# Two attention blocks on one core: where the swapped half of P is put right

## The chip, the core and the metric

The kernel runs on one core of a Trainium2 chip. The metric is the time of one execution on the device in microseconds (us), lower is better. The core has five engines with instruction queues of their own: TensorE (PE; PEld is its weight load), VectorE (DVE), ScalarE (ACT), GpSimd (POOL) and SyncE (SP, which here only issues DMAs). They meet through semaphores.

## The reference

Two attention blocks, A and B, each with its own x, K and V cache and weights, and their outputs side by side. B_x and A_x are 16 x 32 x 1024, all tensors bf16.

```python
def _A_ref(x, k_cache, v_cache, wq, wo):      # Hq = 32, Hkv = 4, Sk = 1024, Dh = 128
    q = (x @ wq).reshape(B, Sq, Hq, Dh).transpose(0, 2, 1, 3)
    k = jnp.repeat(k_cache, rep, axis=1)      # rep = 8
    v = jnp.repeat(v_cache, rep, axis=1)
    scores = jnp.einsum("bhqd,bhkd->bhqk", q, k) * (Dh ** -0.5)
    p = softmax(scores, axis=-1)
    o = jnp.einsum("bhqk,bhkd->bhqd", p, v)
    return o.transpose(0, 2, 1, 3).reshape(B, Sq, Hq * Dh) @ wo
...
return jnp.concatenate([a, b], axis=-1)       # B: the same with 32 K/V heads, no repeat
```

## The kernel before

**Work.** The main loop has 128 steps (NIT). Each does one unit of B, 4 heads of one batch (1 MB of K and 1 MB of V), and one unit of A, half of one K/V head of one batch (256 KB each of K and V for two steps). Between them lie the Q projections (qprojA, qprojB, L660), the output projections (oproj, L716) with their sums in acc (L726, L730), and the loads of the weights.

**One step of B**, in the order of the functions:

- st_dmaK, st_dmaV: SP loads K and V of the 4 heads; partition 32a+p holds 32 keys of head a. There are three slots for each.
- st_ktrB (L844): VectorE transposes K in 32x32 blocks of 4-byte pairs, in two instructions (halves g of the keys), into KBt_sb.
- st_scores (L873, L884): POOL spreads the queries over two columns (QD_sb), and PE makes the scores in 64x64 tiles, each two heads high. Row half r of the array and key half g go to column half cg = r ^ g. So in PSUM the group g=0 has heads 0, 1 on partitions 0 to 63 and heads 2, 3 on 64 to 127, and the group g=1 has them the other way round.
- st_exp (L908): ScalarE makes exp of the scores with the row sums as accumulator output (each such instruction is followed by an accumulator read). For g=0 it is one instruction on 128 partitions. For g=1 there are two on 64 partitions each, which read one half and write P_sb in the other, so that the halves are put right there. L912 ("shift") adds the two row sums on VectorE.
- st_ptr (L920): VectorE transposes P in 32x32 blocks, one instruction of 128x256 for each g, into PT_sb.
- st_pdiag (L933): POOL copies PT_sb into the block-diagonal PD_sb in four copies of 32 partitions. Each needs all of PT_sb, and PD_sb is single.
- st_pv (L981): PE multiplies with V in 64x64 tiles into the banks ps_o and ps_pt.
- st_recip (L990), st_norm (L997, L1001, L1003) and st_otr (L1008, L583): reciprocals of the sums on VectorE, ScalarE brings one bank over (OS_sb), VectorE adds and scales, PE transposes, ScalarE evacuates.

**One step of A:** scores (L862) on PE, one exp of 128x1024 (L899) on ScalarE, PV with a column of ones (L944), and every second step normalisation on VectorE (L954, L956). POOL copies V of A into the tile with the ones (VAp_sb, L819), which frees VA_sb for the next load on SP.

**Order.** The program is first written step by step; then list_schedule puts all operations in an order for each engine by estimated durations (DUR), the longest remaining path, and constants found by tuning (BONUS for each kind of operation, LOOK, A_LEAD, SWITCH_WEIGHT, DMA_MARGIN, SP_AHEAD, slowdown factors). The orders are fixed in the program. Waits are derived from names of buffers and parts of buffers, such as ("P", g, o) or ("PT", g). A second, general program (after L339) runs only where the row sums leave the range, and doesn't run here.

Of the kernel before, what the change touches and what calls it, by code (L numbers as in the profile page):

```python
# [7 lines left out]
ALU = alu_op_type.AluOpType  # L8
ACTF = mybir.ActivationFunctionType
# [10 lines left out]
LAZY_PER_STEP = 100  # L20
LAZY_DELAY = 0
A_STEPS_FRAC = 1.0
LOOK = 0.052
A_LEAD = 577.882
BONUS = {
    "KBt_tr": -157.6, "KTA_ev@act": -282.6, "KTA_ev@dve": -7.6, "KTA_tr": 104.7, "OT_ev@act": 98.0,
    "OT_evA@dve": 194.3, "OT_tr": 55.0, "OT_trA": -66.0, "PD_cp": 120.5, "PD_ev@act": -97.1, "PT_ev@act": -350.3,
    "PT_tr": 47.6, "PT_trB": 28.6, "PVA": -87.3, "PVB": 111.0, "QD_cp": 222.8, "VAp_cp": 84.9, "acc+": 132.0,
    "acc0": 58.0, "accF": -195.1, "exp": -257.9, "expA": 163.5, "ka_dma": 8.8, "kb_dma": 6.2, "norm@dve": -607.1,
    "normA@dve": 228.1, "oprojA": 121.3, "oprojB": -188.6, "oswap": 328.6, "out_dma": 294.6, "qA_ev@act": -27.6,  # L30
    "qA_ev@dve": 383.6, "qB_ev@act": -115.9, "qB_ev@dve": -28.9, "qprojA": 90.7, "qprojB": 150.4, "recip": -7.2,
    "scoresA": -92.9, "scoresB": 19.2, "shift": 89.4, "va_dma": 146.0, "vb_dma": 2.7, "woA_dma": 224.2,
    "woB_dma": 65.7, "wq_dma": 287.0, "xT_ev@act": 434.7, "xT_ev@dve": 233.0, "xT_tr": 131.0, "x_dma": 299.4,
}
SWITCH_WEIGHT = 4.07
DMA_MARGIN = 1.043
PIECE = {"kb_dma": (32768, 32), "wq_dma": (2048, 256), "vb_dma": (32768, 32), "out_dma": (2048, 128)}
PIECE_DEFAULT = (8192, 32)
SP_COST = {"kb_dma": 0.66, "vb_dma": 0.66, "wq_dma": 0.5, "out_dma": 0.5}
SP_COST_DEFAULT = 0.63  # L40
DMA_START = 1.7
SP_AHEAD = 4.874
DMA_LAND = 0.5
DMA_SLOW = 1.06
PE_CLASS = {"scoresB": "S", "PVB": "S"}
PE_LEAVE = {"S": 0.35, "V": 0.16, "F": 0.0}
PE_ENTER = 0.22
PE_SLOW = 1.147
SEEN = {"act": 0.16, "dve": 0.13, "pool": 0.05, "pe": 0.29, "sp": 0.04}

DUR = {
# [30 lines left out]
class Prog:  # L82
# [117 lines left out]
    def list_schedule(self):  # L200
# [40 lines left out]
        while True:  # L241
            best = None
            bkey = None
            for eng, lst in ready.items():
# [6 lines left out]
                emin = min(at.values())  # L251
                ci = max([i for i in lst if at[i] <= emin + LOOK], key=lambda i: (bl[i] + BONUS.get(ops[i].name, 0.0) - SWITCH_WEIGHT * toll(i), -i))
                key = (at[ci], -bl[ci])
# [25 lines left out]
            for u in users[best]:  # L279
                uo = ops[u]  # L280
                r = op.t1 if op.eng == uo.eng == "pe" else seen
                if uo.dma_key is not None:
                    r += DMA_MARGIN
                if r > ready_t[u]:
# [189 lines left out]
def build(nc, pa, pb, out):  # L474
    P = 128
# [9 lines left out]
    scale = float(Dh) ** -0.5  # L485
# [25 lines left out]
    pr = Prog()  # L511
    with contextlib.ExitStack() as stack:
# [3 lines left out]
        def ps(name, shape, dt):  # L516
# [3 lines left out]
        stat = sb("stat", [P, 2, 4], F32)  # L520
        rinv_all = sb("rinv_all", [P, 2 * NIT], F32)
# [9 lines left out]
        acc = sb("acc", [P, 2, NG, D], F32)  # L531
# [9 lines left out]
        PT_sb = sb("PT_sb", [P, Sk // 2], F32)  # L541
# [11 lines left out]
        zeros = PT_sb[:, 0:P // 2].bitcast(BF)  # L553

        ps_s = ps("ps_s", [P, 2, 2, 512], F32)
# [6 lines left out]
        BK_S = [[("bank", 0), ("bank", 1)], [("bank", 2), ("bank", 3)]]  # L562
        BK_KT, BK_PT, BK_O, BK_PJ = ("bank", 4), ("bank", 5), ("bank", 6), ("bank", 7)

        pr.add("pool", lambda g: g.memset(zeros, 0.0), writes=["PT"], name="c0")
        pr.add("pool", lambda g: g.affine_select(ident[:], zeros, [[1, P]], ALU.not_equal, 1.0, base=0, channel_multiplier=-1),
               reads=["PT"], writes=["ident"], name="c1")
        for g in range(2):
# [131 lines left out]
        def oproj(pi, blk, G):  # L700
# [9 lines left out]
            for oh in range(NOH):  # L710
# [17 lines left out]
                else:  # L728
                    claim = ost_claim()
                    pr.add("dve", lambda e, a_ap=a_ap, o_ap=o_ap, ps_a=ps_a: e.tensor_tensor(o_ap, a_ap, ps_a[:, 0:OUTW], ALU.add),  # L730
                           reads=[bk, ("acc", pi, G, oh)] + claim["reads"], writes=[bk, ("ost", ob, oh)] + claim["writes"], name="accF", prio=A_LEAD if pi == 0 else 0.0)
                    if G == NG - 1:
# [161 lines left out]
        def st_exp(q):  # L894
            sbf = q.sbuf
            if q.pi == 0:
                src = ps_s[:, sbf, :, :].rearrange("p u n -> p (u n)")
                dst = PTA_sb[:, q.half, :, :].rearrange("p c n -> p (c n)")
                pr.add("act", lambda e: e.activation(dst, src, ACTF.Exp, scale=scale),  # L899
                       writes=BK_S[sbf] + [("PTA", q.half)], name="expA",  # L900
                       rtag={("Sv", sbf): q.qid}, wtag={("PTA", q.half): q.qid})
            else:
                st = stat[:, q.t % 2, :]
                p_out = P_sb[:, :].rearrange("p (g m j w) -> p g m j w", g=2, m=8, w=2)
                for g in range(2):
                    for o, n, r in (((0, P, 0),), ((0, 64, 64), (64, 64, 0)))[g]:
                        src = ps_s[r:r + n, sbf, g, :].rearrange("p (m w j) -> p m j w", m=8, w=2)
                        pr.add("act", lambda e, src=src, g=g, o=o, n=n: e.activation(p_out[o:o + n, g], src, ACTF.Exp, scale=scale, accum_out=st[o:o + n, g:g + 1]),  # L908
                               writes=[BK_S[sbf][g], ("P", g, o), ("rowsum", q.t % 2, g, o)], name="exp",
                               rtag={("Sv", sbf): q.qid}, wtag={("P", g, o): q.qid, ("rowsum", q.t % 2, g, o): q.qid})  # L910
                parts = [(0, 0), (1, 0), (1, 64)]
                pr.add("dve", lambda e: e.tensor_tensor(st[:, 2:3], st[:, 0:1], st[:, 1:2], ALU.add),  # L912
                       reads=[("rowsum", q.t % 2, g, o) for g, o in parts], writes=[("total", q.t % 2)], name="shift",
                       rtag={("rowsum", q.t % 2, g, o): q.qid for g, o in parts}, wtag={("total", q.t % 2): q.qid})

        def st_ptr(q):
            p32 = P_sb[:, :].bitcast(F32)
            for g in range(2):
                parts = [(0, 0)] if g == 0 else [(1, 0), (1, 64)]
                pr.add("dve", lambda e, g=g: e.transpose(PT_sb[:, 256 * g:256 * g + 256], p32[:, 256 * g:256 * g + 256]),  # L920
                       reads=[("P", g_, o) for g_, o in parts], writes=[("PT", g)], name="PT_tr",
                       rtag={("P", g_, o): q.qid for g_, o in parts}, wtag={("PT", g): q.qid})

        def st_pdiag(q):
            for a in range(4):
                src = PT_sb[32 * a:32 * a + 32, :].rearrange("p (m q) -> p m q", m=16)
                dst = PD_sb[32 * a:32 * a + 32, :, a % 2, :]
                keys = [("PD", a, g) for g in range(2)]
                if a == PD_ACT:
                    pr.add("act", lambda e, src=src, dst=dst: e.copy(dst, src), reads=[("PT", g) for g in range(2)], writes=keys, name="PD_ev@act",  # L930
                           rtag={("PT", g): q.qid for g in range(2)}, wtag={k: q.qid for k in keys})
                else:
                    pr.add("pool", lambda e, src=src, dst=dst: e.tensor_copy(dst, src), reads=[("PT", g) for g in range(2)], writes=keys, name="PD_cp",  # L933
                           rtag={("PT", g): q.qid for g in range(2)}, wtag={k: q.qid for k in keys})

        OA0 = Dh + 4

# [49 lines left out]
                       rtag=dict([(k, q.qid) for k in keys] + [(("VB", kvs), q.kid)]), wtag={"Ops": q.qid})  # L987

        def st_recip(q):
            pr.add("dve", lambda e: e.reciprocal(q.rinv, stat[:, q.t % 2, 2:3]), reads=[("total", q.t % 2)], writes=["rinv", ("rinv_all", 1)], name="recip",  # L990
                   rtag={("total", q.t % 2): q.qid}, wtag={"rinv": q.qid})

        def st_norm(q):
            st = stat[:, q.t % 2, :]
            for o in (0, 64):
                r = 64 - o
                pr.add("dve", lambda e, o=o, r=r: e.reciprocal(st[r:r + 64, 3:4], st[o:o + 64, 2:3]), reads=[("total", q.t % 2)], writes=[("rswap", q.t % 2, r)], name="recip",  # L997
                       rtag={("total", q.t % 2): q.qid}, wtag={("rswap", q.t % 2, r): q.qid})
            for o in (0, 64):
                r = 64 - o  # L1000
                pr.add("act", lambda e, o=o, r=r: e.activation(OS_sb[o:o + 64, :], ps_o1[r:r + 64, 0:Dh], ACTF.Copy, scale=st[r:r + 64, 3:4]),  # L1001
                       reads=[("rswap", q.t % 2, r)], writes=[BK_PT, ("OS", o)], name="oswap", rtag={"Ops": q.qid, ("rswap", q.t % 2, r): q.qid}, wtag={("OS", o): q.qid})
            pr.add("dve", lambda e: e.scalar_tensor_tensor(OB_sb[:, :], ps_o[:, 0:Dh], q.rinv, OS_sb[:, :], ALU.mult, ALU.add),  # L1003
                   reads=["rinv", ("OS", 0), ("OS", 64)], writes=[BK_O, "OB"], name="norm@dve", rtag={"rinv": q.qid, "Ops": q.qid, ("OS", 0): q.qid, ("OS", 64): q.qid}, wtag={"OB": q.qid})
# [168 lines left out]
        pr = pr.list_schedule()  # L1173
# [37 lines left out]
```

## Time and profile before

| what | value |
|---|---|
| time, median of 2 runs | 881.19 us (880.24 to 882.14) |
| the profiled execution | 882.14 us, of which 880.3 us are the span of the profile |
| VectorE: K transposes L844 (KB_sb, wq_sb, xT_sb) | 275.1 + 19.3 + 17.0 us |
| POOL: PD copies L933 | 311.5 us, 512 of 608 ns |
| ScalarE: accumulator reads of L908 | 50.1 + 25.1 us, 384 of 196 ns |
| ScalarE: exp of A, L899 | 131.3 us, 128 of 1025 ns |
| bytes moved | 341.82 MB, mean 388 GB/s |
| mean granted TensorE clock | 0.974 |

The page gives each engine's busy time as a share of the span, then groups of instructions by source line: "x256 | 102.3, 425" reads 256 instructions, 102.3 us busy in all, 425 ns the mean of one; behind the next bar stands the time that the engine was idle just before them, and who ended it. The chain of waits is followed back from the last instruction, at each step to what released it. In the timeline a row begins with its start and its duration in us. The idle time of an engine that sets no pace costs nothing.

### The profile page before, as it was taken

Reading aid. Unit: us, or ns where it says so; the run is one execution under the profiler, and the core shown is the slowest. Engines: PE = TensorE matmul, PEld = TensorE weight load, DVE = VectorE, ACT = ScalarE, POOL = GpSimd, SP = SyncE. Lnnn points to the kernel's source line nnn. Section 1 sums busy time; section 2 is a strip of 40 time slices with the busy share of each in tenths; the row PEclk is TensorE's granted clock in tenths of the full one; section 3 lists DMA queues with packets and bytes.
Section 4 is the critical chain, followed back from the end, with each engine's and each line's share of the span. In section 5 each row is a group of like instructions: output and inputs, shape, how many; then the busy total and the mean of one; then the engine's idle time right before and its main releaser. Section 6 shows DMA issues by size and latency. Waiting matters only on the chain.

```text
span 880.3 us, 32009 instructions
## 1 busy us (share of the span) xinstructions
PE 694.3 (79%) x13529; PEld 422.8 (48%) x13640; DVE 652.7 (74%) x1506; ACT 590.4 (67%) x1365; POOL 458.6 (52%) x716
## 2 busy tenths in 40 slices
PE   3878688887888777888788868887878877677785
PEld 1435455555545444554554535554544545353452
DVE  0685577667867888786878867967878697878784
ACT  1557777677866657677677656757776777676563
POOL 0353555446655555564556445636555475555543
PEclk9999899999999999899999989999999999999797
DMA  8999989899999999899999999989999999999982
GB/s 319 423 427 385 428 321 415 358 370 405 421 404 392 430 421 418 350 390 392 423 424 387 427 427 406 393 335 404 416 396 388 393 422 423 396 372 416 379 349 86
DMA packets 32175, 341.82 MB, mean 388 GB/s; under 512 B 7968, under 2 KB 8480, under 8 KB 17440
## 3 DMA queue, kind: packets, MB, share of 16 engines
q1 hardware_dynamic: 32032, 339.77, 94.8%
q8 instruction: 107, 1.75, 0.7%
q14 instruction: 36, 0.29, 0.1%
HBM read 337.64 MB, written 2.10 MB: 386 GB/s over the span
## 4 chain that ended last, share of the span: by engine, by line
PE 33%; DVE 24%; ACT 20%; POOL 11%; issue 6%; DMA 5%; SPq 0%; POOLq 0%; DVEq 0%; ACTq 0%
ACT P_sb L908 11%; DVE KBt_sb L844 10%; POOL PD_sb L933 8%; PE ps_o L981 8%; PE ps_pj L660 7%; PE ps_s L884 6%; DVE PT_sb L920 4%; PE ps_pj L716 3%; ACT OS_sb L1001 3%; PE ps_kt L944 3%; ACT PTA_sb L899 3%; POOL QD_sb L873 2%; PE ps_s L862 2%; DMA VA_sb<-in_A_v_cache_dram 2%; DVE stat L997 2%
## 5 line engine op out<-in xcount | busy, mean ns | idle before, releaser
L933 POOL COPY PD_sb<-PT_sb 32x512 f32<-32x512 f32 x512 | 311.5, 608 | 262.3 <-PE ps_pt L981 171.0
L844 DVE STREAM_TRANSPOSE KBt_sb<-KB_sb 128x1024 f32<-128x1024 f32 x226 | 275.1, 1231 | 14.0 <-PE ps_s L884 9.7
L908 ACT ACTIVATE P_sb<-ps_s 64x512 bf16<-64x512 f32 (+1 forms) x384 | 228.0, 594 | 48.9 <-PE ps_s L884 19.1
L884 PE MATMUL ps_s<-KBt_sb,QD_sb 64*64 64x512 bf16 x2048 | 149.2, 394 | 33.0 <-ACT P_sb L908 13.0
L981 PE MATMUL ps_o<-VB_sb,PD_sb 64*64 64x128 bf16 x4096 | 146.0, 221 | 32.4 <-POOL PD_sb L933 22.3
L899 ACT ACTIVATE PTA_sb<-ps_s 128x1024 bf16<-128x1024 f32 x128 | 131.3, 1025 | 51.3 <-PE ps_s L862 50.1
L1001 ACT ACTIVATE OS_sb<-ps_pt,stat 64x128 f32<-64x128 f32 x256 | 93.0, 363 | 97.6 <-PE ps_pt L981 92.1
L981 PEld LDWEIGHTS ps_o<-VB_sb,PD_sb 64*64 64x64 bf16 x4096 | 124.7, 109 | 70.0 <-POOL PD_sb L933 42.3
L981 PE MATMUL ps_pt<-VB_sb,PD_sb 64*64 64x128 bf16 x4096 | 146.1, 222 | 2.3 <-issue 2.3
L981 PEld LDWEIGHTS ps_pt<-VB_sb,PD_sb 64*64 64x64 bf16 x4096 | 123.7, 109 | 3.2 <-issue 3.1
L920 DVE STREAM_TRANSPOSE PT_sb<-P_sb 128x256 f32<-128x256 f32 x256 | 102.3, 425 | 25.3 <-POOL PD_sb L933 22.6
L660 PE MATMUL ps_pj<-xT_sb,wq_sb 128*128 128x512 bf16 x416 | 102.5, 386 | 19.4 <-DVE QB_sb L585 5.9
L873 POOL TENSOR_TENSOR QD_sb<-QB_sb,small 128x256 bf16<-128x256 bf16 x128 | 78.5, 613 | 70.4 <-PE ps_s L884 36.0
L819 POOL COPY VAp_sb<-VA_sb 128x1024 bf16<-128x1024 bf16 x64 | 66.4, 1037 | 77.5 <-PE ps_kt L944 41.1
L1003 DVE SCALAR_TENSOR_TENSOR OB_sb<-ps_o,rinv_all,OS_sb 128x128 bf16<-128x128 f32 x128 | 43.4, 339 | 62.9 <-ACT OS_sb L1001 61.7
L884 PEld LDWEIGHTS ps_s<-KBt_sb,QD_sb 64*64 64x64 bf16 x2048 | 52.5, 107 | 72.0 <-DVE KBt_sb L844 12.4
L944 PE MATMUL ps_kt<-VAp_sb,PTA_sb 128*128 128x129 bf16 x1024 | 76.7, 224 | 9.7 <-DVE KTA_sb L585 4.7
L862 PE MATMUL ps_s<-QT_sb,KTA_sb 128*128 128x256 bf16 x512 | 79.3, 277 | 1.0 <-ACT PTA_sb L899 1.0
L944 PEld LDWEIGHTS ps_kt<-VAp_sb,PTA_sb 128*128 128x128 bf16 x1024 | 63.3, 100 | 29.7 <-DVE KTA_sb L585 7.2
L660 PEld LDWEIGHTS ps_pj<-xT_sb,wq_sb 128*128 128x128 bf16 x448 | 44.0, 108 | 68.4 <-issue 9.4
L908 ACT ACTIVATION_READ_ACCUMULATOR P_sb<-ps_s 64x1 f32 (+1 forms) x384 | 75.2, 196 | 1.7
L716 PE MATMUL ps_pj<-woB_sb,OTB_sb 128*128 128x512 bf16 x206 | 58.8, 388 | 11.3 <-ACT OTB_sb L583 6.3
(59 smaller groups left out, 709.2 us busy)
## 6 DMA issues: line engine op xcount, KB each, us to landing
VB_sb<-in_B_v_cache_dram SPq DMA_DIRECT2D x128, 1024.0 KB, 9.6
KB_sb<-in_B_k_cache_dram SPq DMA_DIRECT2D x113, 1024.0 KB, 9.8
VA_sb<-in_A_v_cache_dram SPq DMA_DIRECT2D x64, 256.0 KB, 6.5
KA_sb<-in_A_k_cache_dram SPq DMA_DIRECT2D x64, 256.0 KB, 8.4
wq_sb<-in_B_wq_dram SPq DMA_DIRECT2D x16, 512.0 KB, 9.4
woB_sb<-in_B_wo_dram SPq DMA_DIRECT2D x32, 256.0 KB, 5.3
woA_sb<-in_A_wo_dram SPq DMA_DIRECT2D x32, 256.0 KB, 5.4
wq_sb<-in_B_k_cache_dram SPq DMA_DIRECT2D x8, 1024.0 KB, 11.2
```

Of the source, the lines that this page charges most:

```text
L660: last = e.matmul(ps_pj[:, 0:NTOK], pick(src, j), xT_sb[:, pi, j, :], start=(j == 0), stop=(j == DJ - 1))
L844: pr.add("dve", lambda e: e.transpose(KBt_sb[:, at, :].bitcast(F32).rearrange("p (sh r i) -> p sh r i", sh=4, r=2), k_places[rs][0].bitcas ...
L862: last = e.matmul(ps_s[:, sbf, c2, i * 2 * P:(i + 1) * 2 * P], KTA_sb[:, sl, c * P:(c + 1) * P], qt, start=True, stop=True)
L873: pr.add("pool", lambda e: e.tensor_tensor(QD_sb[:, qd, :, :].rearrange("p f (c q) -> p f c q", c=2), qb.rearrange("p f (c q) -> p f c q", ...
L884: last = e.matmul(ps_s[64 * cg:64 * cg + 64, sbf, g, :].rearrange("p (sh i) -> p sh i", sh=4), QD_sb[64 * r:64 * r + 64, qd, fp, :], kt[g] ...
L899: pr.add("act", lambda e: e.activation(dst, src, ACTF.Exp, scale=scale), writes=BK_S[sbf] + [("PTA", q.half)], name="expA", rtag={("Sv", s ...
L908: pr.add("act", lambda e, src=src, g=g, o=o, n=n: e.activation(p_out[o:o + n, g], src, ACTF.Exp, scale=scale, accum_out=st[o:o + n, g:g + 1]),
L920: pr.add("dve", lambda e, g=g: e.transpose(PT_sb[:, 256 * g:256 * g + 256], p32[:, 256 * g:256 * g + 256]), reads=[("P", g_, o) for g_, o ...
L933: pr.add("pool", lambda e, src=src, dst=dst: e.tensor_copy(dst, src), reads=[("PT", g) for g in range(2)], writes=keys, name="PD_cp", rtag ...
L944: last = e.matmul(ps_kt[:, qh * OA0:qh * OA0 + Dh + 1], PTA_sb[:, h, c, qh * P:(qh + 1) * P], VAp_sb[:, sl, 4 * h + c, 0:Dh + 1], start=(h ...
L981: last = e.matmul(acc_[64 * cg:64 * cg + 64, 0:Dh], pd[64 * r:64 * r + 64, m, :, w], VB_sb[64 * r:64 * r + 64, kvs, 8 * sh + 4 * g + 2 * c ...
L1001: pr.add("act", lambda e, o=o, r=r: e.activation(OS_sb[o:o + 64, :], ps_o1[r:r + 64, 0:Dh], ACTF.Copy, scale=st[r:r + 64, 3:4]), reads=[(" ...
```

## The change

The two 64-partition exps of g=1 become one of 128 partitions that leaves the halves swapped; P_sb then holds group g=1 with swapped halves. The P transpose of g=1 is cut into two of 64 partitions that read one half and write the other. The row sums of g=1 now lie on the other half, so the addition is cut into two of 64 partitions that take one operand from each half. The parts' names follow, and the waits with them. All constants of the scheduler named in the diff get other values, so that the order of the instructions changes on every engine. Lines behind st_exp move up by two.

```diff
-LOOK = 0.052
-A_LEAD = 577.882
+LOOK = 0.1
+A_LEAD = 110.269
...
-SWITCH_WEIGHT = 4.07
-DMA_MARGIN = 1.043
+SWITCH_WEIGHT = 77.91
+DMA_MARGIN = 2.952
...
-SP_AHEAD = 4.874
+SP_AHEAD = 4.171
...
-DMA_SLOW = 1.06
+DMA_SLOW = 1.071
...
-PE_SLOW = 1.147
+PE_SLOW = 1.176
...
                 for g in range(2):
-                    for o, n, r in (((0, P, 0),), ((0, 64, 64), (64, 64, 0)))[g]:
-                        src = ps_s[r:r + n, sbf, g, :].rearrange("p (m w j) -> p m j w", m=8, w=2)
-                        pr.add("act", lambda e, src=src, g=g, o=o, n=n: e.activation(p_out[o:o + n, g], src, ACTF.Exp, scale=scale, accum_out=st[o:o + n, g:g + 1]),
...
-                pr.add("dve", lambda e: e.tensor_tensor(st[:, 2:3], st[:, 0:1], st[:, 1:2], ALU.add),
...
+                    src = ps_s[:, sbf, g, :].rearrange("p (m w j) -> p m j w", m=8, w=2)
+                    pr.add("act", lambda e, src=src, g=g: e.activation(p_out[:, g], src, ACTF.Exp, scale=scale, accum_out=st[:, g:g + 1]),
...
+                for i in range(2):
+                    o, r = 64 * i, 64 * (1 - i)
+                    pr.add("dve", lambda e, o=o, r=r: e.tensor_tensor(st[o:o + 64, 2:3], st[o:o + 64, 0:1], st[r:r + 64, 1:2], ALU.add),
...
-            for g in range(2):
-                parts = [(0, 0)] if g == 0 else [(1, 0), (1, 64)]
-                pr.add("dve", lambda e, g=g: e.transpose(PT_sb[:, 256 * g:256 * g + 256], p32[:, 256 * g:256 * g + 256]),
...
+            for g, o, n, r in ((0, 0, P, 0), (1, 0, 64, 64), (1, 64, 64, 0)):
+                pr.add("dve", lambda e, g=g, o=o, n=n, r=r: e.transpose(PT_sb[o:o + n, 256 * g:256 * g + 256], p32[r:r + n, 256 * g:256 * g + 256]),
```

The values of BONUS change for nearly all kinds of operation (exp from -257.9 to -155.8, shift from 89.4 to 6.4, PT_tr from 47.6 to 11.0, KBt_tr from -157.6 to -84.8, norm@dve from -607.1 to -371.1, for example). POOL's copies wait for all three parts of PT_sb, as they waited for both before.

## The prediction

> **What bounds the kernel now.** I read the page's head, the DMA queues and the chain first.
>
> ```profile
> span 880.3 us, 32009 instructions
> ...
> PE 694.3 (79%) x13529; PEld 422.8 (48%) x13640; DVE 652.7 (74%) x1506; ACT 590.4 (67%) x1365; POOL 458.6 (52%) x716
> ...
> q1 hardware_dynamic: 32032, 339.77, 94.8%
> ...
> PE 33%; DVE 24%; ACT 20%; POOL 11%; issue 6%; DMA 5%; SPq 0%; POOLq 0%; DVEq 0%; ACTq 0%
> ```
>
> The three DMA queues together (94.8, 0.7 and 0.1%) are busy for 95.6% of 880.3 us: 841.6 us of transfers, 39 us without. No engine is over 79%, and the chain of waits has every engine in it, so the engines are a ring that keeps up with DMA. The busy times in stretches of 20 us show where it doesn't:
>
> ```profile
> core 0: us, PE busy (x) PEld busy (x) DVE busy (x) ACT busy (x) POOL busy (x), PEclk, DMA share, GB/s
> 560.00:580.00 20.00, 15.80 (x263) 9.15 (x258) 18.07 (x41) 12.22 (x30) 11.21 (x17) 1.00 1.00 413
> 580.00:600.00 20.00, 18.50 (x344) 11.32 (x345) 12.25 (x30) 13.88 (x29) 8.22 (x13) 1.00 0.85 306
> 700.00:720.00 20.00, 16.34 (x328) 9.37 (x328) 18.76 (x43) 15.43 (x38) 11.11 (x18) 1.00 1.01 427
> 860.00:880.00 20.00, 9.93 (x229) 5.55 (x228) 7.58 (x27) 6.03 (x18) 5.51 (x10) 0.70 0.21 74
> ```
>
> Two kinds of stretch are to be seen. At 580, with projections, PE is at 18.5 of 20 and DMA falls to 0.85: PE sets the pace. At 560 and 700 DMA is full (413 and 427 GB/s) and DVE is at 18.07 and 18.76 of 20: nearly a second bound. Idle DMA is 3.0 us in the first 20 us (share 0.85), 15.8 in the last 20 (0.21), and about 16 at places like 580. So even a kernel whose engines never hold DMA up in the middle would need some 841.6 + 3.0 + 15.8 = 860 us.
>
> **The terms' rows**, with shapes kept apart:
>
> ```profile
> L908 ACT ACTIVATE P_sb<-ps_s 64x512 bf16<-64x512 f32 x256 | 151.5, 592 | 33.6 <-PE ps_s L884 16.5 <-DVE PT_sb L920 4.8 <-DVE stat L997 1.5
> ...
> L908 ACT ACTIVATE P_sb<-ps_s 128x512 bf16<-128x512 f32 x128 | 76.5, 598 | 15.3 <-DVE PT_sb L920 8.2 <-PE ps_s L884 2.6 <-PE ps_pt L981 1.6
> ...
> L920 DVE STREAM_TRANSPOSE PT_sb<-P_sb 128x256 f32<-128x256 f32 x256 | 102.3, 425 | 25.3 <-POOL PD_sb L933 22.6 <-ACT OTB_sb L583 1.0 <-ACT P_sb L908 0.9
> ...
> L912 DVE TENSOR_TENSOR stat<-stat 128x1 f32<-128x1 f32 x128 | 36.1, 282 | 39.2 <-ACT P_sb L908 38.5
> ```
>
> **ScalarE: one exp a step fewer.** An exp on 64 partitions takes 592 ns, on 128 598: the width in partitions is free, so two full exps do the work of three. Their distance when nothing is in the way, each with its accumulator read, is read from the timeline:
>
> ```profile
> 709.85 0.59 ACT L908 ACTIVATE P_sb<-ps_s 64x512 bf16<-64x512 f32 x1
> ...
> 710.56 0.60 ACT L908 ACTIVATE P_sb<-ps_s 128x512 bf16<-128x512 f32 x1
> ...
> 711.27 0.59 ACT L908 ACTIVATE P_sb<-ps_s 64x512 bf16<-64x512 f32 x1
> ```
>
> That is 0.71 us each, so 128 x 0.71 = 91 us leave ScalarE (busy 590 to about 500). What it buys in time: at 700 ScalarE is at 15.4 of 20, at 580 at 13.9, so it sets the pace in neither; the 11% of the chain on L908 is a ring's share and would pass to what is next late. I take 3 us off (0 to the 16 us of idle DMA in the middle).
>
> **VectorE: one P transpose a step more, and none that joins.** The third transpose is 64x256, a shape with no row. By the exp rows the width is free, so 425 ns (half of it, 0.21, as the lower bound). Today the two transposes mostly overlap: two in a row take 0.77 us, so the second costs 0.34. A pair of 64-row reciprocals that changes half (L997, 156 ns each) takes 0.34 to 0.35 us, that is, nothing overlaps. If so, three cost 3 x 0.43 + 0.05 = 1.34 against 0.77: +0.57; if they still joined, +0.34; with the lower bound of duration +0.2. I take +0.50, nearer to the reciprocals, which change half in the same way: 128 x 0.50 = 64 us. The Trainium skill, "VectorE: DVE Perf Modes", section "Two Vector instructions with no wait between them", speaks against the change here: an instruction whose input or output starts in another group of 32 partitions than the last one's is held until all earlier ones have finished. By it the sum would take +0.57 and be 9 us of DVE higher; no run here shows it for transposes.
>
> **VectorE: two row-sum additions in place of one.** L912 has a least time of 116 ns, a median of 160, a mean of 282 and a most of 1045. The long ones end when a POOL copy does:
>
> ```profile
> 102.65 1.04 POOL L819 COPY VAp_sb<-VA_sb 128x1024 bf16<-128x1024 bf16 x1
> ```
> ```profile
> 103.00 0.70 DVE L912 TENSOR_TENSOR stat<-stat 128x1 f32<-128x1 f32 x1
> ```
>
> Both end at 103.69 to 103.70. So an addition of two SBUF operands seems to wait for POOL's running copy, on average 0.12 us. The new one costs 0.19 (the distance of the reciprocals) and a wait of its own: 0 to a whole PD copy, 0.61. In the new instruction order 46 of the 128 first additions stand directly behind the last P transpose, which is what releases POOL's copies; today most stand in front of the pair (82 of 128). I take 0.35 a step (0.19 + 0.12 and a little for that place), bounds 0.19 and 0.80: 45 us. Behind a waiting addition on DVE stand the reciprocals and the K transposes, which free K slots for SP's loads.
>
> DVE's sum: 652.7 + 64 + 45 = 762 us, 86% of the span; at the bounds 0.4 a step 704, and 1.37 a step 828.
>
> **Latency from scores to P's copies.** Exp loses 0.71, the transposes behind the last exp gain 0.45: -0.26 us a step. POOL's four copies now need all three transposes, as they needed both before; they mostly wait for PV (171 us of waits on L981), which covers it: nothing. SP's longest wait, 246.7 us for L819, stands behind those copies on POOL; loads land 6 to 10 us after issue, which hides a shift of some tenths: nothing. The re-tuned constants re-order every queue; PE's matmuls and all loads keep their number and size, so I cost the order at nothing, +-8 us as the scatter between two such orders (half of the 16 us of idle DMA in the middle).
>
> **What DVE's 0.85 us a step costs in time.** In each stretch I add 0.85 times its steps (half the P transposes in it) to DVE's busy time and call what exceeds 18.76 of 20, the fullest stretch of this trace, overload. At 700: 18.76 + 4 x 0.85 = 22.16, 3.4 us over; at 560: 18.07 + 3.5 x 0.85 = 21.05, 2.3 over. Over all stretches of 20 us it is 24 us; in stretches of 40 us, where neighbours even it out, 4 us. Three K and three V slots hold about three steps, or 20 us, so the truth lies between; I take 10. Sum: 882.1 (this execution) + 10 - 3 = 889 us, and by the medians of the two runs (881.2 against 882.1) 888.
>
> **Rivals.**
> - *DVE becomes the bound* (slower). With 1.1 to 1.37 a step the overload of the 40 us stretches is 18 to 43 us, of the 20 us ones 41 to 64. It needs the additions to wait for a whole POOL copy in most steps. For it speaks the new place of 46 additions; against it the 171 us in which POOL waits for PV, so that a copy often doesn't start at once. It decides from about 1.1 us a step. Time 882 + 30 = 912, up to 930.
> - *ScalarE's relief pays* (not slower). DVE's idle time is 227 us, of which 62 wait for L1001 and 38.5 for L908, both of ScalarE; an earlier exp could give that back, and DVE's extra 109 us fits into it. Then DMA stays the bound and some of its 16 us is won: 882 - 9 = 873, 866 at best. Against it: at 560 and 700 DVE has hardly any idle time left.
> - *The exps don't get fewer*: excluded, the instruction lists have 256 full exps in place of 384.
>
> **Chances.** Forecast (880 to 899, likeliest 888) 0.50; DVE as the bound 0.31; relief 0.19. Range 868 to 918: it leaves out the best third of the relief case and the worst third of the DVE case and some order scatter. Bound of 2%, about what these runs tell from no change: 863.6 and 898.8. Faster by over 2% is at the very floor of 860: 0.04. Slower: the DVE case and the upper edge of the forecast, 0.33. The rest, 0.63, within.
>
> **What would show it.** ScalarE near 500 us and 256 exps of 598 ns; the 64x256 transposes at about 430 ns and three of them 1.3 us end to end; additions of over 0.5 us that end with a POOL copy; DVE at 740 to 790 us; DMA at about 94.5% and, in the stretches with four steps in 20 us, below 1.0, with DVE above 19. It is wrong if 64-row transposes take half as long, if DVE stays under 720 us, or if the stretches that lose DMA are those of the projections.

## The result, and the profile after

| | before | after |
|---|---|---|
| time, median of 2 runs | 881.19 us (880.24 to 882.14) | 950.23 us (950.18 to 950.28) |
| ratio | 1 | 1.078, interval 1.073 to 1.083 |
| span of the profiled execution | 880.3 us | 948.4 us |
| VectorE / ScalarE busy | 652.7 / 590.4 us | 767.9 / 482.7 us |
| mean granted TensorE clock | 0.974 | 0.949 |

The change makes the kernel 7.8% slower; 888 us, with a range of 868 to 918, had been predicted. The page of after, its head, the largest DMA queue and the chain of waits:

```profile
span 948.4 us, 32077 instructions
...
PE 717.0 (76%) x13526; PEld 431.8 (46%) x13640; DVE 767.9 (81%) x1762; ACT 482.7 (51%) x1109; POOL 457.6 (48%) x716
...
q1 hardware_dynamic: 32032, 339.77, 91.5%
...
DVE 51%; PE 25%; ACT 8%; POOL 7%; issue 7%; DMA 1%; SPq 0%; POOLq 0%; DVEq 0%; ACTq 0%
```

VectorE has 115 us more work and carries 51% of the chain (before 24%). ScalarE has 108 us less and falls from 20% of the chain to 8%. The queue was busy for 94.8% of 880.3 us before, and is now for 91.5% of 948.4, so I read that DMA no longer sets the pace. VectorE's idle time is 948.4 - 767.9 = 180.5 us, against 227.6 before, so only 47 of the 115 us went into idle time; 68 us lengthened the span.

The operations that the change touches, by line with shapes kept apart (busy us, mean ns, then idle time and who ended it):

```profile
L931 POOL COPY PD_sb<-PT_sb 32x512 f32<-32x512 f32 x512 | 310.8, 607 | 345.9 <-PE ps_pt L979 200.8 <-DVE PT_sb L919 81.3 <-PE ps_s L884 12.4
L907 ACT ACTIVATE P_sb<-ps_s 128x512 bf16<-128x512 f32 x256 | 151.8, 596 | 99.8 <-DVE PT_sb L919 64.0 <-PE ps_s L884 25.2 <-PE ps_kt L942 2.0
L919 DVE STREAM_TRANSPOSE PT_sb<-P_sb 64x256 f32<-64x256 f32 x256 | 112.6, 440 | 8.7 <-ACT P_sb L907 0.5
L912 DVE TENSOR_TENSOR stat<-stat 64x1 f32<-64x1 f32 x256 | 66.4, 259 | 16.8 <-ACT P_sb L907 8.1
L919 DVE STREAM_TRANSPOSE PT_sb<-P_sb 128x256 f32<-128x256 f32 x128 | 54.9, 429 | 16.7 <-POOL PD_sb L931 12.2 <-ACT P_sb L907 2.9 <-ACT PTA_sb L899 0.8
```

The full exps cost 596 ns as before. A transpose on 64 partitions takes 440 ns, as long as one on 128. The exps now wait 64.0 us for the P transposes that free P_sb (before 16.5 + 8.2 in the two groups of exps), and POOL's copies 81.3 us (before 31.3). The relieved engine stands waiting for the loaded one. POOL's copies in before:

```profile
L933 POOL COPY PD_sb<-PT_sb 32x512 f32<-32x512 f32 x512 | 311.5, 608 | 262.3 <-PE ps_pt L981 171.0 <-DVE PT_sb L920 31.3 <-PE ps_s L884 12.7
```

How the transposes and additions lie, in the timeline of VectorE (start, length, the instruction; "x3" joins three of a line):

```profile
403.56 0.91 DVE L919 STREAM_TRANSPOSE PT_sb<-P_sb 64x256 f32<-64x256 f32 x2
404.50 0.65 DVE L912 TENSOR_TENSOR stat<-stat 64x1 f32<-64x1 f32 x2
...
418.74 1.37 DVE L919 STREAM_TRANSPOSE PT_sb<-P_sb 128x256 f32<-128x256 f32 x3
```

In before a pair stands together so:

```profile
419.09 0.76 DVE L920 STREAM_TRANSPOSE PT_sb<-P_sb 128x256 f32<-128x256 f32 x2
```

Three transposes take 1.37 us where the pair, partly joined, took 0.76, a difference of 0.61; two of 64 partitions take 0.91, a little over twice their 0.44: nothing overlaps. The two additions of 404.50 take 0.65 us, though the median of one is 155 ns. Beside them, in POOL's timeline:

```profile
404.53 1.27 POOL L931 COPY PD_sb<-PT_sb 32x512 f32<-32x512 f32 x2 [1.14 <-DVE PT_sb L919]
```

By the mean of 607 ns the first of these two copies runs from 404.53 to about 405.14, and the additions end at 405.15. Last, the busy times in stretches of 20 us:

```profile
core 0: us, PE busy (x) PEld busy (x) DVE busy (x) ACT busy (x) POOL busy (x), PEclk, DMA share, GB/s
...
580.00:600.00 20.00, 15.71 (x339) 9.73 (x340) 16.99 (x38) 10.96 (x25) 10.21 (x16) 1.00 0.84 318
700.00:720.00 20.00, 14.03 (x213) 7.77 (x217) 17.51 (x39) 7.38 (x18) 8.66 (x13) 1.00 0.95 357
780.00:800.00 20.00, 12.26 (x311) 8.23 (x311) 19.13 (x42) 10.87 (x25) 11.73 (x19) 1.00 0.97 389
```

At 780 VectorE does 19.13 of 20, more than the 18.76 that I had taken for its capacity. At 580 and 700 it does 16.99 and 17.51, and DMA is at 0.84 and 0.95 there too: time is lost where no engine is full.

### The profile page after: what moved, and what is told of

Read it like the earlier page. It is cut to its first block, busy times and chain, and to the rows that moved or that the text cites. A ratio compares the mean times of both kernels' runs of the same rounds, so it can differ in the third digit from the quotient of the medians.

```text
span 948.4 us, 32077 instructions
## 1 busy us (share of the span) xinstructions
PE 717.0 (76%) x13526; PEld 431.8 (46%) x13640; DVE 767.9 (81%) x1762; ACT 482.7 (51%) x1109; POOL 457.6 (48%) x716
## 3 DMA queue, kind: packets, MB, share of 16 engines
q1 hardware_dynamic: 32032, 339.77, 91.5%
## 4 chain that ended last, share of the span: by engine, by line
DVE 51%; PE 25%; ACT 8%; POOL 7%; issue 7%; DMA 1%; SPq 0%; POOLq 0%; DVEq 0%; ACTq 0%
DVE KBt_sb L844 20%; DVE PT_sb L919 11%; PE ps_o L979 6%; POOL PD_sb L931 6%; DVE stat L912 5%; PE ps_pj L660 5%; PE ps_pj L716 4%; PE ps_s L884 4%; ACT P_sb L907 3%; DVE OB_sb L1001 3%; DVE acc L726 3%; DVE stat L995 3%; ACT OS_sb L999 2%; PE ps_s L862 2%; ACT PTA_sb L899 2%
## 5 line engine op out<-in xcount | busy, mean ns | idle before, releaser
L907 ACT ACTIVATE P_sb<-ps_s 128x512 bf16<-128x512 f32 x256 | 151.8, 596 | 99.8 <-DVE PT_sb L919 64.0
L919 DVE STREAM_TRANSPOSE PT_sb<-P_sb 64x256 f32<-64x256 f32 (+1 forms) x384 | 167.4, 436 | 25.3 <-POOL PD_sb L931 12.2
L979 PE MATMUL ps_o<-VB_sb,PD_sb 64*64 64x128 bf16 x4096 | 153.0, 228 | 30.7 <-POOL PD_sb L931 13.8
L979 PEld LDWEIGHTS ps_o<-VB_sb,PD_sb 64*64 64x64 bf16 x4096 | 132.0, 114 | 70.8 <-issue 33.4
L979 PE MATMUL ps_pt<-VB_sb,PD_sb 64*64 64x128 bf16 x4096 | 153.2, 229 | 1.6 <-issue 1.5
L979 PEld LDWEIGHTS ps_pt<-VB_sb,PD_sb 64*64 64x64 bf16 x4096 | 130.9, 114 | 2.2 <-issue 2.0
L660 PE MATMUL ps_pj<-xT_sb,wq_sb 128*128 128x512 bf16 x415 | 103.8, 390 | 17.2 <-DVE acc L726 6.2
L583 ACT COPY OTB_sb<-ps_o 128x128 bf16<-128x128 bf16 x128 | 33.9, 265 | 146.4 <-PE ps_o L1006 145.9
L942 PE MATMUL ps_kt<-VAp_sb,PTA_sb 128*128 128x129 bf16 x1024 | 72.4, 221 | 11.0 <-DVE KTA_sb L585 6.7
L912 DVE TENSOR_TENSOR stat<-stat 64x1 f32<-64x1 f32 x256 | 66.4, 259 | 16.8 <-ACT P_sb L907 8.1
L1006 PE MATMUL ps_o<-ident,OB_sb 128*128 128x128 bf16 x128 | 29.2, 228 | 62.3 <-DVE OB_sb L1001 61.8
```

What stands on the lines that cost most here:

```text
L660: last = e.matmul(ps_pj[:, 0:NTOK], pick(src, j), xT_sb[:, pi, j, :], start=(j == 0), stop=(j == DJ - 1))
L907: pr.add("act", lambda e, src=src, g=g: e.activation(p_out[:, g], src, ACTF.Exp, scale=scale, accum_out=st[:, g:g + 1]), writes=[BK_S[sbf] ...
L912: pr.add("dve", lambda e, o=o, r=r: e.tensor_tensor(st[o:o + 64, 2:3], st[o:o + 64, 0:1], st[r:r + 64, 1:2], ALU.add), reads=[("rowsum", q ...
L919: pr.add("dve", lambda e, g=g, o=o, n=n, r=r: e.transpose(PT_sb[o:o + n, 256 * g:256 * g + 256], p32[r:r + n, 256 * g:256 * g + 256]), rea ...
L942: last = e.matmul(ps_kt[:, qh * OA0:qh * OA0 + Dh + 1], PTA_sb[:, h, c, qh * P:(qh + 1) * P], VAp_sb[:, sl, 4 * h + c, 0:Dh + 1], start=(h ...
L979: last = e.matmul(acc_[64 * cg:64 * cg + 64, 0:Dh], pd[64 * r:64 * r + 64, m, :, w], VB_sb[64 * r:64 * r + 64, kvs, 8 * sh + 4 * g + 2 * c ...
```

## The experiments

Two theories stood at the start. LOAD (in the expectations mostly "Theory DVE"): VectorE's added work costs time wherever it lies. ORDER: the re-tuned constants put the instructions in a bad order, and the arithmetic is nearly free. A third, RING, came later: the chain exp, P transposes, POOL's copies, PV, whose buffers are single, has become longer, and work elsewhere on VectorE would cost little.

**Is it the order?** Two runs: the change's code with before's constants, and before's code with the change's.

```diff
e1:  after, but LOOK, A_LEAD, BONUS, SWITCH_WEIGHT, DMA_MARGIN, SP_AHEAD, DMA_SLOW, PE_SLOW as in before
e2:  before, but all of these as in after
```

> The code of the change, with the scheduler's constants of the kernel before. Theory ORDER (the re-tuned constants give a bad order and make most of the 69 us): near 890 to 900 us, with VectorE's busy time still about 765. Theory DVE (VectorE's extra 115 us are the bound, whatever the order): 935 to 965 us, and VectorE again the largest share of the chain of waits.

> The code of before, with the re-tuned constants of the change. Theory ORDER: 930 to 950 us, with VectorE's busy time still about 653. Theory DVE: within 880 to 900 us, the scatter between two orders.

Measured: 950.44 us (1.079, interval 1.068 to 1.089) and 940.18 us (1.067, 1.050 to 1.085). With before's constants the change is as slow as with its own, so they are not why it lost. But the change's constants on before's code cost 59 us with no engine busier (VectorE 649.8, ScalarE 592.5 us). Its waits show where:

```profile
L933 POOL COPY PD_sb<-PT_sb 32x512 f32<-32x512 f32 x512 | 311.2, 608 | 341.3 <-PE ps_pt L981 270.4 <-DVE stat L912 23.4 <-DVE PT_sb L920 8.1
...
L908 ACT ACTIVATE P_sb<-ps_s 128x512 bf16<-128x512 f32 x128 | 76.5, 598 | 45.1 <-DVE PT_sb L920 40.1 <-PE ps_s L884 2.3 <-PE ps_kt L962 0.5
```

POOL waits 270 us for PV in place of 171; my reading, which no run tested, is that PV stands too late on PE's list. So the change's constants are no better for the change than before's are, and much worse for before's code. A later run took only part of them over:

```diff
e9:  before, but LOOK, A_LEAD, SWITCH_WEIGHT, DMA_MARGIN, SP_AHEAD, DMA_SLOW, PE_SLOW as in after; BONUS unchanged
```

> Before, with the change's values of LOOK, A_LEAD, SWITCH_WEIGHT, DMA_MARGIN, SP_AHEAD, DMA_SLOW and PE_SLOW, and the BONUS values of before. e2, with both, lost 57 us at an unchanged VectorE. If the margins and slowdown factors make that order: 920 to 945 us. If the BONUS values make it: 880 to 900. Either way VectorE stays near 650 us busy.

912.09 us (1.036, 1.029 to 1.044), between the two ranges: some half of the 59 us comes with these values. That the rest comes with BONUS is inferred; BONUS alone was not run.

**Would the planner do better if it knew the true durations?**

```diff
 # after, before's constants (as e1), and in DUR:
-    "PT_tr": 0.36,   "shift": 0.1,
+    "PT_tr": 0.45,   "shift": 0.25,
```

> The code of the change with the scheduler's constants of before, and with the durations that were measured in the profile after (P transpose 0.45 in place of 0.36, addition 0.25 in place of 0.1), so that the planner knows what VectorE costs. Theory ORDER in the form that the planner's wrong durations make the order bad: 895 to 915 us. Theory DVE: 935 to 955, as e1.

970.32 us (1.097, 1.082 to 1.113), 20 us worse than e1, VectorE 762.2 us. A miss for the thought that a wrong estimate in the plan was the cause.

**The parts alone, on before.** The third transpose without a swap, and the two exps without the swap:

```diff
 # e5: three exps as before; the transpose of g=1 is cut, each piece keeps its half
-            for g in range(2):
+            for g, o, n in ((0, 0, P), (1, 0, 64), (1, 64, 64)):
...
+                pr.add("dve", lambda e, g=g, o=o, n=n: e.transpose(PT_sb[o:o + n, 256 * g:256 * g + 256], p32[o:o + n, 256 * g:256 * g + 256]),
```
```diff
 # e6: two exps on 128 partitions, transposes and addition as in before; the halves stay swapped
-                    for o, n, r in (((0, P, 0),), ((0, 64, 64), (64, 64, 0)))[g]:
-                        src = ps_s[r:r + n, sbf, g, :].rearrange("p (m w j) -> p m j w", m=8, w=2)
+                    src = ps_s[:, sbf, g, :].rearrange("p (m w j) -> p m j w", m=8, w=2)
+                    pr.add("act", lambda e, src=src, g=g: e.activation(p_out[:, g], src, ACTF.Exp, scale=scale, accum_out=st[:, g:g + 1]),
```

> Before, with one edit: the second P transpose of 128x256 is cut into two of 64x256 that read and write the same half (nothing is swapped, the exps stay three). It prices the third transpose alone. Theory DVE: VectorE's busy time rises by 128 x 0.57 = 73 us, and the time by a good half of the loss, 25 to 50 us: 905 to 930. Theory ORDER: the same busy time, but 880 to 895 us.

> Before, with one edit: the exps in two full instructions a step, and nothing that puts the halves of g=1 right again: P of that group is multiplied with the V of the other pair of heads, and its row sums go to the wrong half (this part is left out). It prices ScalarE's relief alone. If ScalarE's share of the chain (20%) is worth something by itself: 865 to 875 us. If DMA and VectorE set the pace: 876 to 884, with ScalarE's busy time down by 95 to 105 us.

e5: 933.06 us (1.059, 1.045 to 1.073), just above the range of LOAD. VectorE has 709.3 us, 57 more than before (73 had been expected), and the time grows by 52, at an unchanged number of exps. But a piece more in the plan gives another order, so a share of the 52 may be the order's. Without the swap three transposes in a row take less than the 1.37 us of after:

```profile
304.93 1.23 DVE L920 STREAM_TRANSPOSE PT_sb<-P_sb 128x256 f32<-128x256 f32 x3
```

So 0.47 of the 0.61 us comes with the cut, and 0.14 with the swap.

e6: 871.95 us (0.987, 0.984 to 0.990) with ScalarE at 477.0 us: taking 113 us off ScalarE buys 9 us by the medians, 12 by the ratio.

**The parts in one order.** From here the order is held fixed: e6's plan is kept on every engine, and where the change has two or three instructions for one, they stand together in that one's place. e8 has all of the change's arithmetic; e8b only its three transposes, e8c only its two additions.

```diff
 # e8b and e8: on e6
-                pr.add("dve", lambda e, g=g: e.transpose(PT_sb[:, 256 * g:256 * g + 256], p32[:, 256 * g:256 * g + 256]),
+                    for o, n, r in (((0, P, 0),), ((0, 64, 64), (64, 64, 0)))[g]:
+                        last = e.transpose(PT_sb[o:o + n, 256 * g:256 * g + 256], p32[r:r + n, 256 * g:256 * g + 256])
 # e8c and e8: on e6
-                pr.add("dve", lambda e: e.tensor_tensor(st[:, 2:3], st[:, 0:1], st[:, 1:2], ALU.add),
+                    for o, r in ((0, 64), (64, 0)):
+                        last = e.tensor_tensor(st[o:o + 64, 2:3], st[o:o + 64, 0:1], st[r:r + 64, 1:2], ALU.add)
```

> The arithmetic of the change (two exps, three P transposes of which two swap, two crosswise row-sum additions), planned like e6: the two swapping transposes are one operation for the scheduler, and so are the two additions, so that the order on PE, ScalarE, POOL and SP is that of e6, and on VectorE too but for the doubled instructions. Theory DVE (its 115 us of extra work cost the time, whatever the order): 925 to 955 us. Theory ORDER (the plan is what costs): 875 to 890 us.

> As e8, but with the one addition of before (the row sums of g=1 are added on the wrong half, so the normalisation differs from the reference). It prices the third, swapping transpose in the plan of e6. Theory DVE: 128 x 0.57 = 73 us of VectorE, and the larger part of the loss, 905 to 935 us. Theory ORDER: 873 to 882.

> As e8, but with the two P transposes of before (P of g=1 keeps its halves swapped, so it meets the V of the other pair of heads). It prices the second addition in the plan of e6: 0.2 to 0.3 us a step, 25 to 40 us of VectorE. Theory DVE: 885 to 900 us. Theory ORDER: 873 to 880.

**Or the ring?** r1 leaves P alone and puts the same amount of work on K: the first K transpose of each step is cut in three.

```diff
 # r1: on e6
+                if t_ == 1:
+                    return e.transpose(dst, src)
+                e.transpose(dst[:, 0:2], src[:, 0:2])
+                e.transpose(dst[0:64, 2:4], src[0:64, 2:4])
+                return e.transpose(dst[64:128, 2:4], src[64:128, 2:4])
```

r2 is e8 with the additions in another form, the second row sum as a scalar of each partition:

```diff
-                        last = e.tensor_tensor(st[o:o + 64, 2:3], st[o:o + 64, 0:1], st[r:r + 64, 1:2], ALU.add)
+                        last = e.tensor_scalar(st[o:o + 64, 2:3], st[o:o + 64, 0:1], st[r:r + 64, 1:2], None, ALU.add)
```

> The kernel with two exps and the swap left out (871.95 us, VectorE 647.8), in its own order of instructions on every engine, plus VectorE work away from P: the first K transpose of each step is cut into three instructions (128 partitions for two of the four stretches, and 64 + 64 partitions for the other two). By the rows seen, that is +0.8 to +0.9 us a step, about 110 us of VectorE, as much as the change's extra transposes and additions cost there (766.0 - 647.8 = 118). P, PT_sb and PD_sb are untouched. Theory LOAD (VectorE's busy time itself is what costs, wherever it lies): 930 to 955 us, as the whole change in this order (951.6). Theory RING (the chain exp, P transposes, POOL's copies, PV, each with one buffer, is what costs when it gets longer): 872 to 895 us, VectorE near 755 to 765 all the same. Between 900 and 925: both have a part.

> The change's arithmetic in the order of the kernel with two exps (951.6 us, VectorE 766.0), with the two crosswise additions written with the second row sum as a scalar per partition, so that by the run on before's addition they no longer wait for POOL's running copy (mean 200 ns there, never over 215). Theory that the wait of the additions for POOL is what the second addition costs: VectorE some 15 to 35 us less, 925 to 940 us. Theory that the additions cost by their own length and their place in front of the P transposes: 945 to 955 us. If it ends below 908 (the run with the swapping transposes alone), the additions cost nothing else than that wait.

All six have one order. VectorE's time is that of the profiled execution; the times are medians of 2 or 3 runs, e6's of 8:

| run | VectorE busy, us | over e6 | time, us | over e6 | us of time per us of VectorE | ratio to before |
|---|---|---|---|---|---|---|
| e6 | 647.8 | | 871.95 | | | 0.987 [0.984, 0.990] |
| e8c, additions | 693.4 | +45.6 | 897.44 | +25.5 | 0.56 | 1.015 [1.001, 1.029] |
| e8b, transposes | 718.7 | +70.9 | 908.22 | +36.3 | 0.51 | 1.027 [1.015, 1.039] |
| r2, both, other additions | 751.6 | +103.8 | 931.87 | +59.9 | 0.58 | 1.054 [1.047, 1.061] |
| r1, K transposes | 753.4 | +105.6 | 941.85 | +69.9 | 0.66 | 1.069 [1.058, 1.079] |
| e8, the change | 766.0 | +118.2 | 951.60 | +79.7 | 0.67 | 1.076 [1.064, 1.089] |

The change costs the same 950 to 952 us in three orders (its own, e1's, e6's; in e4's it costs 970). Its two parts make 25.5 + 36.3 = 62 us alone and 80 together; with intervals of some 11 us each, it stays open whether they cost more together. r1 decides between the theories: RING had said 872 to 895, LOAD 930 to 955, and the same work put on K gives 942. No place makes VectorE's work cheap; it costs 0.5 to 0.7 us of time per us of work. Two sections show how. Each goes from one exp of A to the eighth after it, with six steps of B in the first and eight in the second, so that but for the added work the same lies in all three kernels. The columns are as in the stretches above; e6 first:

```profile
140.20:179.45 39.25, 36.78 (x683) 22.12 (x684) 28.72 (x74) 26.10 (x58) 21.21 (x32) 1.00 0.92 358
692.75:740.83 48.08, 38.59 (x880) 23.19 (x877) 40.11 (x97) 28.06 (x68) 29.74 (x47) 0.96 1.01 422
```

The same two sections of e8, the change:

```profile
151.25:198.15 46.90, 38.61 (x683) 22.69 (x684) 35.09 (x84) 26.29 (x58) 22.02 (x33) 0.96 0.86 323
752.17:805.92 53.75, 38.65 (x880) 23.66 (x879) 47.31 (x114) 28.22 (x69) 29.53 (x46) 0.97 0.94 381
```

And of r1, the work on K:

```profile
149.03:193.44 44.41, 36.84 (x683) 22.13 (x684) 33.66 (x84) 26.18 (x58) 22.08 (x34) 1.00 0.89 343
742.71:797.74 55.03, 38.35 (x880) 23.26 (x877) 47.28 (x112) 28.23 (x68) 29.68 (x47) 0.97 0.92 369
```

The first section is PE's: in e6 PE is busy for 36.78 of 39.25 us, VectorE for 28.72, 73%. By a count of VectorE's capacity its 10.5 us of idle time would have taken the 6.4 us that the change adds. In r1, at the same clock of PE, VectorE gets 4.9 us more work there and the section takes 5.2 us more. In e8 it takes 46.90 us, 7.65 more, with VectorE at 75%; 1.8 of these are PE's own, at a clock of 0.96. The second section is DMA's in e6 (share 1.01), with VectorE at 83%; with 7.2 us more work it takes 5.7 us more in e8, and 7.0 in r1. So VectorE's idle time was hardly slack. The waits of the first section say why. A row gives who waits for whom, the us in all, how often, and the longest; first e6, then e8, then r1:

```profile
DVE OB_sb L1000 <- ACT OS_sb L998: 7.2, 4, 3.9
PE ps_o L1005 <- DVE OB_sb L1000: 0.4, 2, 0.3
```
```profile
DVE OB_sb L1008 <- ACT OS_sb L1006: 6.9, 3, 3.9
PE ps_o L1013 <- DVE OB_sb L1008: 3.2, 2, 2.3
```
```profile
DVE OB_sb L1007 <- ACT OS_sb L1005: 6.9, 4, 3.9
PE ps_o L1012 <- DVE OB_sb L1007: 3.5, 2, 2.1
```

VectorE's largest wait there, for OS_sb, which ScalarE copies from PE's result, stays at 7 us of its 10.5 us of idle time: the added work doesn't go into it. In its place PE waits longer for what VectorE makes: with all such rows 1.1 us in e6, 7.0 in e8 and 6.5 in r1. Over the whole run it is the same (sums of PE's waits for VectorE of more than 0.15 us, in the profiled execution):

| run | PE's waits for VectorE, us | over e6 | PE busy, us | over e6 | time over e6 |
|---|---|---|---|---|---|
| e6 | 87.5 | | 715.3 | | |
| e8c | 113.5 | +26.0 | 718.1 | +2.8 | +25.5 |
| e8b | 125.3 | +37.8 | 716.7 | +1.4 | +36.3 |
| r2 | 150.7 | +63.2 | 725.1 | +9.8 | +59.9 |
| r1 | 161.7 | +74.2 | 723.5 | +8.2 | +69.9 |
| e8 | 154.5 | +67.0 | 733.7 | +18.4 | +79.7 |

So most of the added time is time in which PE waits for VectorE. PE's own busy time adds 1 to 18 us for the same matmuls, at a lower granted clock (0.967 in e6, 0.945 in e8). From before to after PE's waits for VectorE rise from 84.6 to 146.2 us, with 68 us more of span.

**Is it VectorE alone?** The swap can be made in POOL's copies, which leaves VectorE near e6's time (642.4 us).

```diff
 # v2: on e6; the row sums of g=1 are swapped by POOL too, and two durations of POOL's operations in DUR follow
+                    for g in range(2):
+                        s = a ^ (2 * g)
+                        last = e.tensor_copy(dst[:, 8 * g:8 * g + 8, :], PT_sb[32 * s:32 * s + 32, 256 * g:256 * g + 256].rearrange("p (m q) -> p m q", m=8))
```

> Two exps and two whole P transposes, as in e6, but the swapped half is put right by POOL: each of its four copies is cut in two of 32x256, and those of g=1 read the other half; POOL also swaps the row sums of g=1 in two small copies, so that VectorE keeps one addition. The result is the reference's. Theory DVE (VectorE's work is what costs, POOL has room at 52%): VectorE near 650 us of busy time, POOL up by 50 to 90 us, 870 to 885 us. If the place of the swap costs by its longer path to PV, whichever engine does it: 900 or more.

927.67 us (1.055, 1.052 to 1.059): LOAD's 870 to 885 is missed, and POOL's added time with it (136 us for 50 to 90; half a copy takes 392 ns, a whole one 608). Its busy times and chain:

```profile
PE 704.5 (76%) x13527; PEld 423.8 (46%) x13640; DVE 642.4 (70%) x1506; ACT 477.4 (52%) x1109; POOL 594.0 (64%) x1484
...
POOL 37%; PE 28%; DVE 18%; issue 8%; ACT 5%; DMA 4%; SPq 0%; POOLq 0%; DVEq 0%; ACTq 0%
```

POOL got 136 us more than in e6 and no engine is over 76%, yet 56 us of time are added, 0.41 per us of POOL. POOL's share of the chain is 37%, in e6 9%, so it looks as if POOL's work had a price too. How much isn't shown: this plan's order is not e6's, and an order alone cost 59 us above.

**The additions.** e11 is before with only its addition in the form of r2, in before's order.

```diff
-                pr.add("dve", lambda e: e.tensor_tensor(st[:, 2:3], st[:, 0:1], st[:, 1:2], ALU.add),
+                pr.add("dve", lambda e: e.tensor_scalar(st[:, 2:3], st[:, 0:1], st[:, 1:2], None, ALU.add),
```

> Before, with one edit at the same order: the row-sum addition takes its second operand as a per-partition scalar, so that it reads one tensor in place of two. It tests whether the addition's long times are a wait for POOL's copy that hangs on the second tensor. If so, its mean falls from 282 ns to 150 to 170 and its most from about 1 us to under 0.2; VectorE's busy time falls by about 15 us, and with the price that e6 and e8c show for VectorE (about 0.6 us of time for 1 us of its work) the time falls by 5 to 10 us, to 872 to 878. If the wait has another cause, the times of the addition stay and the time is 878 to 885.

Time 880.84 us (0.999, 0.996 to 1.003). The line's least, median and longest ns, in before, in e11, in after and in r2:

```profile
L912 DVE TENSOR_TENSOR stat<-stat x128: 116/160/1045, 36.1 to 866.3; 128x1 f32<-128x1 f32 x128
```
```profile
L912 DVE TENSOR_SCALAR stat<-stat x128: 170/212/215, 35.4 to 866.8; 128x1 f32<-128x1 f32 x128
```
```profile
L912 DVE TENSOR_TENSOR stat<-stat x256: 153/155/1006, 37.2 to 935.3; 64x1 f32<-64x1 f32 x128
```
```profile
L912 DVE TENSOR_SCALAR stat<-stat x256: 207/209/213, 34.2 to 919.7; 64x1 f32<-64x1 f32 x128
```

The form with a scalar is a third slower at the median (212 against 160 ns, 209 against 155), and its longest is 215 ns; the other's is over 1 us. By the traces, 51 of before's 128 additions take over 250 ns, and each of these ends within 0.04 us of the end of a POOL instruction; in e11 45 lie wholly inside a POOL instruction and don't wait for its end. On before this saves VectorE 11 us and buys nothing in time, where 5 to 10 us had been expected. On the change it saves 14 us, and the time falls from 951.6 to 931.9, as the theory of the wait had said (925 to 940); that this is more than 0.7 per us lies within the intervals (11 and 6 us). My reading of the difference is that before is at DMA's limit (95.6% with all queues) and the change is not. v2 with this addition gave 929.58 us, no gain there either. In v2 no addition had taken over 356 ns, and VectorE's busy time went up with the slower form, from 642.4 to 648.0 us:

> v2 with the addition of e11 (second operand as a scalar). If e11's edit frees VectorE of a wait for POOL: 5 to 10 us below v2, 862 to 878. If not, the same as v2 within 3 us.

## Why the prediction was wrong, step by step

- **What bounds the kernel.** "A ring that keeps up with DMA" fits what followed, and the sum did not use it: it looked for stretches in which VectorE alone is full.
- **ScalarE's relief, 3 us (0 to 16).** Its busy time fell by 108 us to 482.7, where 91 and "about 500" had been said: 0.84 us a step, not 0.71. e6 measures the relief alone, its new order counted in, at 9 us by the medians (881.2 - 871.95) and 12 by the ratio: more than the 3 taken, within the bounds. (The 16 us of idle DMA that made this bound, and half of which made the +-8 of the order, are rather 39 - 3.0 - 15.8 = 20; the miss doesn't hang on that.)
- **The third transpose, +0.50 a step.** e8b measures 70.9 / 128 = 0.55, and three in a row differ from the pair by 0.61. By the rule of the Trainium skill that I weighed, "VectorE: DVE Perf Modes", section "Two Vector instructions with no wait between them", my estimate was +0.57. The three transposes of 1.37 us agree with the rule, and so do the 1.23 us of e5, where only the last of the three starts in another group of partitions; the measured 0.55 is nearer to that estimate than to my 0.50.
- **The second addition, +0.35 a step.** e8c measures 45.6 / 128 = 0.36. The reason given, a wait for POOL's running copy, stands too: the wait goes with the second SBUF tensor operand (e11, r2). The Trainium skill, same page and section, says that the second SBUF read interface is shared with GpSimd. The longest addition of 1045 ns with two tensors, and of 215 with a tensor and a scalar, fit that.
- **VectorE's sum, 762 us.** Measured 767.9.
- **The failed step: "What DVE's 0.85 us a step costs in time".** The amount was right (0.90 measured), its conversion to time wrong. I took 18.76 of 20 us as VectorE's capacity, called only what exceeds it overload, and got 10 us for 109 us of work, 0.09 per us. The one-order runs show 0.51 to 0.67 per us. The assumption behind it, that a stretch's idle time on VectorE takes in new work, is what the sections refute: where VectorE was at 73%, 4.9 us of work on K cost 5.2 us, and 6.4 us of the change's cost 7.65. What they show in its place: VectorE's idle time there is mostly a wait for ScalarE's copy that stays, and the added work makes PE wait for VectorE, 67 us more in e8 and 74 in r1 over the whole run. In hindsight, with e6 as the start and the mean of the five prices, 0.60, e8's 118 us of work give 872 + 0.60 x 118 = 943 us; as e8 is one of the five, this checks the size and forecasts nothing.
- **"The order at nothing, +-8".** The bound was far too narrow: the new constants cost before's code 59 us. It is not why this result was missed, since the change takes 950 us in three orders (and 970 in e4's).
- **Latency at nothing.** POOL's wait for PV was to cover the later transposes. It did only in part: POOL's waits for P transposes rose from 31.3 to 81.3 us. But r1, which doesn't touch that chain, has the same (from 20.2 in e6 to 56.2) and costs as much per us, so this wait is no price of its own.
- **The rivals.** "DVE becomes the bound" (912, up to 930) ends on the right side, for another reason: its condition, additions that wait for a whole copy in most steps and 1.1 us a step, was not met (259 ns on average, 0.90 us), and its price used the same conversion. "Relief pays" (873) fits e6, which leaves the added work out, and failed with it.
- **What was to show it.** ScalarE, the transposes, the additions and VectorE's sum showed as written. The DMA share near 94.5% did not (91.5% for the largest queue, 92.3% for all three), and DMA is lost also where VectorE is below 18 of 20.

What stays open is why PE's clock and busy time go along with the time, and which buffers tie VectorE's results to PE so closely. Second buffers for P_sb or PT_sb weren't tried. Of the kernels that leave no part out, none is faster than before (e11 is as fast); e6, at 872 us, is what a free swap would reach in its order.

## What to carry to other kernels

In this kernel three engines at 65 to 80% wait for each other in fixed orders, and the idle time of VectorE was no reserve: 1 us of added work cost 0.5 to 0.7 us. Work taken away with DMA at 95% bought little (0.89 us a step off ScalarE some 10 us, where 0.92 a step more on VectorE cost 80). For a kernel like it this is a better first estimate than counting only what exceeds an engine's fullest stretch; that it holds elsewhere isn't shown. Before calling an engine's idle time slack, look at what it waits for, and at who waits for that engine. Hold the order of instructions fixed when the parts of such a change are measured, since the order alone moved this kernel by up to 59 us.

## What the runs showed of the hardware that I had not expected

- The mean granted TensorE clock is mostly lower in the slower kernels, by spans: 0.974 at 880 us, 0.964 and 0.965 at 898 and 906 (e8c and e8b), 0.954 at 940 (r1), 0.949 and 0.945 at 948 and 950 (after, e8), 0.939 at 972 us (e4). It isn't strict: 0.967 at 873 (e6), 0.957 at 950 (e1). PE's busy time says how much of the price this can be, 1 to 18 us; which of the two causes the other wasn't tested.
- Cutting a transpose costs a whole one even if both pieces keep their partitions: in e5 the 64x256 pieces without a swap took 420 ns, those with the swap 440, and three in a row 1.23 against 1.37 us.
